# GQA decode attention with a small MLP on one core: all engines synchronized by hand in one section, TensorE's head groups in a loop, each loaded weight used by two matmuls

## The chip, the core and the metric

The kernel runs on one core of a Trainium2 chip. A core has TensorE (PE; its weight loads are counted apart, as PEld), VectorE (DVE), ScalarE (ACT), GpSimd (POOL), SyncE (SP, which here only issues DMAs), and 16 DMA engines that move data between HBM and the on-chip memory SBUF. The metric is the device time of one execution in microseconds (us). All runs quoted here are of the state called fast. A profile's span is about 1.8 us shorter than the time of the same execution, because it starts at the first instruction and ends with the last; times and spans are not mixed below.

## The reference, cut to what matters

```
B, Sq, D = 2, 1, 512
Hq, Hkv, Sk, Dh = 32, 8, 32768, 128            # 4 query heads share one K/V head
q = (x @ wq) ... ; scores = q . k * Dh**-0.5 ; p = softmax(scores) ; o = p . v
s = o.reshape(B, Sq, Hq * Dh) @ wo
g = silu(mlp(x))                                # small: 512 -> 1792 -> 512
return x + s * g
```

K and V hold 2 x 8 x 32768 x 128 bf16 elements each, 134 MB each. With wq, w3, w4 and wo the kernel must read 280.5 MB. There are 16 head groups (a batch and a K/V head), of 8.39 MB of K and 8.39 MB of V each. K arrives with its rows on the partitions; both kernels transpose it in SBUF on DVE before TensorE multiplies it with q (291.5 us of DVE in the kernel before).

## The kernel before

A framework places buffers in pools and derives the waits. K lies in a ring of three half-group slots, V in two. Per group there are two halves; each half takes eight transposes on DVE, 32 score matmuls, one exp, and 32 products with V. The finish of each group follows it at once.

```
kbuf = rings.tile([128, 3 * SLOT], BF16, name="kbuf")      # SLOT = 128 rows x 128, 32 KB a partition
vbuf = rings.tile([128, 2 * SLOT], BF16, name="vbuf")
...
for r in range(NR):                                        # emit_k: 8 chunks a half
    T = ktp.tile([128, W], I32, tag="T", name="T")         # 4 buffers of 1,024 words
    nc.vector.transpose(out=T..., in_=kt[:, r * W:(r + 1) * W]...)
    for nb in range(NB):
        for e in range(2):
            nc.tensor.matmul(sc[:, :], lhsT=z[:, nb, e, zc:zc + 128], rhs=Tb[:, nb, :, e], ...)
...                                                        # emit_v, last half of a group
nc.scalar.copy(out=ob[:, :], in_=o[:, :])
for t in range(VT):
    nc.tensor.matmul(oT[:, :], lhsT=ob[:, t * Dh:(t + 1) * Dh], rhs=sel_o[:, t, :], ...)
...                                                        # divide, select, put into oX
wo_parts = [(0, 4), (4, 7), (7, 8)]
for m in range(NG):
    eps = [emit_k(m, hs[0], True)]
    if not last: load_k(*groups[m + 1], ...)               # issued by SP
    eps.append(emit_k(m, hs[1], False))
    for i in range(NPART): emit_v(m, hs[i], i, eps[i])
    if not last: load_v(*groups[m + 1], ...)
    if m == NG - 2: ...                                    # wo, in wo_parts, behind the last K and V
```

The softmax here doesn't subtract the row's maximum and nothing guards it: scores larger than these inputs give would overflow.

## Time and profile before

| | before |
|---|---|
| time, median | 660.65 us (660.59 to 660.91, 3 runs) |
| span | 658.9 us |
| DMA | 280.91 MB, 426 GB/s over the span |
| PE busy, DVE busy | 59%, 53% |

These lines are from the page of the kernel before: busy time by engine, then the span in 40 slices (the digit is the busy share in tenths), then the busy share and the rate of the DMA engines in each slice, and the queues (queue, kind: packets, MB, share of 16 engines).

```profile
PE 386.7 (59%) x2652; PEld 172.1 (26%) x2684; DVE 346.0 (53%) x442; ACT 50.3 (8%) x152; POOL 6.9 (1%) x20
...
DMA  9999999999999999999999999999999999999995
GB/s 367 451 426 442 435 446 439 410 443 426 439 438 435 430 435 422 447 434 423 442 427 442 438 419 434 443 434 443 414 423 446 443 442 443 410 427 428 431 421 224
...
q1 hardware_dynamic: 6408, 280.50, 98.6%
q8 instruction: 21, 0.34, 0.2%
```

Read this as: no engine of the core is near full, the DMA engines are (9 tenths or more in every slice but the last). Queue 8 carries instructions, in 21 packets of 16 KB (below, "fetches").

The next lines are the chain of waits of the kernel before, in order of time (start, duration, what), cut to two groups and the end.

```profile
2.13 40.20 DMA kbuf<-in_A_k_cache_dram
...
51.51 29.45 DMA kbuf<-in_A_k_cache_dram
...
90.14 29.41 DMA kbuf<-in_A_k_cache_dram
...
613.66 39.09 DMA kbuf<-in_A_wo_dram
652.79 1.90 PE s_ps L400 x63
```

By these lines K tiles land at 42.33, 80.96 and 119.55 us, 38.6 us apart, which is 16.78 MB (K and V of a group) at about 434.6 GB/s. The end hangs on the load of wo, not on the last scores. The timeline of the finish (start, duration, instruction, in brackets the idle time before it and what ended that) shows why: the last V half is multiplied as soon as the last of its 16 completions is in (they come from 639.54 to 644.11 us, the products start at 644.15), the group's own finish is done at 650.2, and PE then waits for wo.

```profile
637.87 0.71 DVE L322 STREAM_TRANSPOSE pt<-ep 128x512 bf16<-128x512 bf16 x1 [1.87 <-ACT ep L320]
639.07 1.90 PE L343 MATMUL o<-vbuf,pt 128*16 128x512 bf16 x32
644.15 3.38 PE L343 MATMUL o<-vbuf,pt 128*16 128x512 bf16 x32 [3.18 <-DMA vbuf<-in_A_v_cache_dram]
650.01 0.17 DVE L372 TENSOR_REDUCE oX<-xm 128x4 bf16<-128x16 f32 x1
652.79 1.88 PE L400 MATMUL s_ps<-kbuf,oX 128*2 128x128 bf16 x64 [2.00 <-DMA kbuf<-in_A_wo_dram]
655.43 0.66 SPq L412 DMA_DIRECT2D out_dram<-out  x1
```

### The profile page before, as it was taken

The numbers are of one execution on the slowest core, as the hardware profiler recorded it, in microseconds if no ns is written. First come the engines' busy times: TensorE is split into PE (matmuls) and PEld (weight loads), VectorE is DVE, ScalarE is ACT, GpSimd is POOL, SyncE is SP. The second block draws the span as 40 slices with busy tenths as digits, with TensorE's granted clock in tenths as the row PEclk, the third lists the DMA queues.
The fourth block names the chain that finished last, engine by engine and source line by source line (L and its number), as shares of the span: only waits on it lengthen the run. The fifth ranks groups of instructions, "written<-read, shape, count | busy, mean of one in ns | idle before, by whom it ended". The sixth has DMA issues, their size and how long they took to land.

```text
span 658.9 us, 6323 instructions
## 1 busy us (share of the span) xinstructions
PE 386.7 (59%) x2652; PEld 172.1 (26%) x2684; DVE 346.0 (53%) x442; ACT 50.3 (8%) x152; POOL 6.9 (1%) x20
## 2 busy tenths in 40 slices
PE   2338194673828557283764729377482946738764
PEld 2313132231313223131331313123131322313322
DVE  5147192754809265381935629183572918447560
ACT  1301001010100101000010100101010010100000
POOL 4000000000000000000000000000000000000000
PEclk9999688786968968697886959878596877859896
DMA  9999999999999999999999999999999999999995
GB/s 367 451 426 442 435 446 439 410 443 426 439 438 435 430 435 422 447 434 423 442 427 442 438 419 434 443 434 443 414 423 446 443 442 443 410 427 428 431 421 224
DMA packets 6704, 280.91 MB, mean 426 GB/s; under 512 B 906, under 2 KB 916, under 8 KB 1940
## 3 DMA queue, kind: packets, MB, share of 16 engines
q1 hardware_dynamic: 6408, 280.50, 98.6%
q8 instruction: 21, 0.34, 0.2%
q0 software_dynamic: 256, 0.01, 0.0%
q14 instruction: 7, 0.06, 0.0%
q10 hardware_dynamic: 12, 0.00, 0.0%
HBM read 280.50 MB, written 0.00 MB: 426 GB/s over the span
## 4 chain that ended last, share of the span: by engine, by line
DMA 75%; DVE 14%; issue 7%; PE 3%; SPq 0%; ACT 0%; DVEq 0%
DMA kbuf<-in_A_k_cache_dram 69%; DVE T L303 14%; DMA kbuf<-in_A_wo_dram 6%; PE sc L311 2%; PE o L343 1%; PE s_ps L400 0%; ACT ep L320 0%; SPq L95 0%; DVE pt L322 0%; SPq L115 0%; SPq L392 0%; SPq L114 0%; SPq L101 0%; PE S L339 0%; DVE sg L408 0%
## 5 line engine op out<-in xcount | busy, mean ns | idle before, releaser
L311 PE MATMUL sc<-T,z 128*128 128x512 bf16 x992 | 276.4, 421 | 206.3 <-DVE T L303 197.8
L303 DVE STREAM_TRANSPOSE T<-kbuf 128x1024 int32<-128x1024 int32 x256 | 291.5, 1205 | 150.5 <-DMA kbuf<-in_A_k_cache_dram 150.5
L311 PEld LDWEIGHTS <-z 128*128 128x128 bf16 x1024 | 105.7, 103 | 371.2 <-issue 278.7
L343 PE MATMUL o<-vbuf,pt 128*16 128x512 bf16 x1024 | 69.9, 434 | 3.2 <-DMA vbuf<-in_A_v_cache_dram 3.2
L320 ACT ACTIVATE ep<-sc 128x512 bf16<-128x512 f32 x32 | 19.1, 597 | 493.2 <-PE sc L311 451.2
L334 DVE MEMSET o<- 128x512 f32 x16 | 7.8, 485 | 69.3 <-ACT ob L352 68.3
L322 DVE STREAM_TRANSPOSE pt<-ep 128x512 bf16<-128x512 bf16 x32 | 22.6, 707 | 34.7 <-ACT ep L320 34.4
L343 PEld LDWEIGHTS <-pt 128*16 128x16 bf16 x1024 | 27.2, 99 | 37.9 <-issue 18.2
L339 PE MATMUL S<-sm,ones_f 128*128 128x4 f32 x64 | 10.7, 238 | 26.1 <-DVE sm L338 26.1
L355 PE MATMUL oT<-sel_o,ob 128*128 128x4 f32 x128 | 16.9, 255 | 11.1 <-ACT ob L352 11.1
L355 PEld LDWEIGHTS oT<-sel_o,ob 128*128 128x128 f32 x128 | 15.5, 191 | 19.3 <-ACT ob L352 19.3
L339 PEld LDWEIGHTS S<-sm,ones_f 128*128 128x128 f32 x64 | 10.7, 188 | 30.9 <-DVE sm L338 28.4
L352 ACT COPY ob<-o 128x512 f32<-128x512 f32 x16 | 9.4, 586 | 83.4 <-PE o L343 83.4
L362 DVE TENSOR_TENSOR on<-oT,rec 128x4 bf16<-128x4 f32 x16 | 2.6, 162 | 21.8 <-PE oT L355 21.8
L286 ACT COPY z<-qr 32x16 bf16<-32x16 bf16 x64 | 12.6, 198 | 11.5 <-DVE qr L233 10.9
L360 DVE RECIPROCAL rec<-S 128x4 f32<-128x4 f32 x16 | 2.9, 182 | 7.6 <-PE S L339 7.6
L365 PEld LDWEIGHTS <-sel_r 128*128 128x128 bf16 x64 | 5.2, 117 | 5.2 <-issue 5.2
L320 ACT ACTIVATION_READ_ACCUMULATOR ep<-sc 128x1 f32 x32 | 6.3, 198 | 0.2
L215 PE MATMUL qT_ps<-xT,kbuf 128*128 128x2 bf16 x128 | 3.6, 165 | 4.5 <-DMA kbuf<-in_A_wq_dram 4.5
L365 PE MATMUL xp<-on,sel_r 128*128 128x4 bf16 x64 | 3.8, 164 | 4.1 <-DVE on L362 4.1
L338 DVE TENSOR_SCALAR sm<-sel_h,rs 128x4 f32<-128x4 f32 x32 | 6.0, 188 | 0.0
L370 DVE TENSOR_TENSOR xm<-xp,mask 128x16 f32<-128x16 f32 x16 | 2.8, 174 | 5.3 <-PE xp L365 5.3
(64 smaller groups left out, 48.5 us busy)
## 6 DMA issues: line engine op xcount, KB each, us to landing
kbuf<-in_A_k_cache_dram SPq DMA_DIRECT2D x2, 4096.0 KB, 29.1
vbuf<-in_A_v_cache_dram SPq DMA_DIRECT2D x2, 4096.0 KB, 26.7
kbuf<-in_A_wq_dram SPq DMA_DIRECT2D x1, 4096.0 KB
vbuf<-in_B_w_dram SPq DMA_DIRECT2D x2, 1792.0 KB, 21.6
kbuf<-in_A_wo_dram SPq DMA_DIRECT2D x1, 2048.0 KB, 35.9
kbuf<-in_A_wo_dram SPq DMA_DIRECT2D x1, 1536.0 KB, 39.1
kbuf<-in_A_wo_dram SPq DMA_DIRECT2D x1, 512.0 KB
kbuf<-in_A_k_cache_dram SPq DMA_DIRECT2D x15, 29.4
```

Of the source, the lines that this page charges most:

```text
L286: nc.scalar.copy(out=z[32 * j:32 * j + 32, :, :, c:c + rep], in_=qr[32 * j:32 * j + 32, :, :, b, g * rep:(g + 1) * rep],)
L303: nc.vector.transpose(out=T[:, :].rearrange("p (b t k) -> p t b k", b=NB, t=RT), in_=kt[:, r * W:(r + 1) * W].rearrange("p (t b k) -> p t ...
L311: nc.tensor.matmul(sc[:, :], lhsT=z[:, nb, e, zc:zc + 128], rhs=Tb[:, nb, :, e], start=(r == 0 and nb == 0 and e == 0), stop=(r == NR - 1 ...
L320: nc.scalar.activation(out=ep[:, :], in_=sc[:, :], func=ACT.Exp, scale=inv_sqrt_dh, accum_out=rs[:, :])
L322: nc.vector.transpose(out=pt[:, :, :].rearrange("p r (t h) -> p t r h", h=rep), in_=ep[:, :].rearrange("p (t r h) -> p t r h", r=NR, h=rep),)
L334: nc.vector.memset(state["o"][:, :], 0.0)
L338: nc.vector.tensor_scalar_mul(out=sm[:, :], in0=sel_h[:, :], scalar1=rs[:, 0:1])
L339: nc.tensor.matmul(S[:, :], lhsT=ones_f[:, :], rhs=sm[:, :], start=(i == 0), stop=(i == NPART - 1))
L343: nc.tensor.matmul(o[32 * j:32 * j + VT * rep, :], lhsT=pt[:, r, a * VT * rep:(a + 1) * VT * rep], rhs=vt[:, u * VT:(u + 1) * VT, :].rearr ...
L352: nc.scalar.copy(out=ob[:, :], in_=o[:, :])
L355: nc.tensor.matmul(oT[:, :], lhsT=ob[:, t * Dh:(t + 1) * Dh], rhs=sel_o[:, t, :], start=(t == 0), stop=(t == VT - 1),)
L365: nc.tensor.matmul(xp[:, r, :], lhsT=sel_r[:, r, :, :].rearrange("p j w -> p (j w)"), rhs=on[:, :], start=True, stop=True,)
```

## The change

The intent is fewer instructions and fewer weight loads. The kernel is rewritten as one section in which every wait is written by hand. PE's work for the first 15 groups becomes a loop of 197 instructions. One transpose covers 2,048 words, one exp covers a whole group, and a loaded weight serves two matmuls. The group's output is masked and reduced on DVE (collect), and the selection sums over all groups are done once, behind the last group's scores. wo comes in four parts. The diff rewrites nearly the whole file; its core:

```
-    kbuf = rings.tile([128, 3 * SLOT], BF16, name="kbuf")
+    kbuf = stile([128, 3 * UNIT], BF16, "kbuf")           # now the first buffer of the program
+    T = [stile([128, W], I32, f"T{i}") for i in range(2)] # 2 buffers of 2,048 words
...
+    with nc.Fori(1, NG, engines=bass.OrderedEngineSet([PE]), head_slot={PE: 0}) as i:
+        nc.tensor.wait_ge(s_z, i)
+        for n in range(NR):
+            nc.tensor.wait_ge(s_T[n], i)
+            emit_chunk(n)            # 4 x (ldweights, then 2 matmuls that use it)
+        nc.tensor.wait_ge(s_pt, i)
+        nc.tensor.wait_ge(s_v[0], i * 16)
+        pe.done(emit_v(0, NU))
...
+    for m in range(NL):              # NL = 15
+        k_read = scores(m)           # transposes, exp, transpose of p; issues K(m + 1)
+        t_ob.append(collect(m, t_v(m)))   # DVE: mask multiply and reduce, 128x1024
+        sp.wait(t_v(m))
+        V.append(load_v(m + 1))
...
+    for n in range(NR):              # the last group
+        pe.wait((s_T[n], NG))
+        emit_chunk(n)
+    scores(m)
+    t_sm = weigh(0, NL)
+    t = sums(0, NL, t_sm, t_ob[-1], ...)   # PE: 1 + 15 f32 matmuls
+    t_on = divide(0, NL, t, ...)
+    t_sm = weigh(NL, NG)
+    pe.wait(t_pt[-1], V[m][0])
+    emit_v(0, NU // 2)
...
-    wo_parts = [(0, 4), (4, 7), (7, 8)]
+    wo_parts = [(0, 2), (2, 5), (5, 7), (7, 8)]
```

## The prediction

> **What bounds it now.** The DMA stream. The page shows DMA at 9 tenths or more in every slice but the last; its chain of waits is 75% DMA; PE is busy 59%, DVE 53%. In the chain of waits K tiles land every 38.6 us (42.35, 80.98, 119.57, ...): 16.78 MB (K and V of one head group) per 38.6 us = 434.6 GB/s. The packet records agree: 64 KB takes 2,418 ns on one of 16 engines. [...] 280.5 MB at that rate is an estimated 646 us of 658.9. The queue never runs dry: the next K is issued 9 us after K lands, with about 10 us of V still in flight. So only the head, the tail and time lost inside the stream can move.
>
> **Lost time.** The packet records show 21 instruction fetches of 16 KB on queue 8, and some of 8 KB on queue 14. Each 16 KB fetch (about 0.9 us) also lengthens that DMA engine's next data packet by about 0.5 us: 1.4 us on one engine. Engines are hit two or three times, and a load is complete only when its slowest engine is. The spread between first and last engine grows from 0.63 us (first load) to 4.5 us (last V). [...]
>
> **What the change does.**
> - PE's program falls from 5,090 to 700 instructions as built[...]. DVE falls from 662 to 252. Nearly all fetches vanish: the last V lands near 640 to 641 us instead of 643.7, wo near 650 instead of 652.8: -2.8 us, all on the critical path.
> - Halved weight loads (105.7 us in L311, 27.2 us in L343), wider transposes and exps: less PE, DVE and ACT work, none on the path: 0.
> - T has two buffers of 2,048 columns, not four of 1,024: K's first half is read in 10 to 12 us, inside V's 19.3 us. No new wait.
> - Tail: after wo's landing 16 matmuls (about 0.5 us) are left in place of 64 (1.9 us): -1.3 us. The last group's finish gains DVE work (mask multiply and reduction over 128x1024, about 1.1 us each, estimated from the trace's 128x512 and 128x1024 instructions): 9 us after V lands against 6.5, but wo comes 9 us after V: a near tie.
> - [...]
>
> Sum: 660.65 - 2.8 - 1.3 + 0.6 = about 657.1 us, 0.5% faster.
>
> **Predicted: 657.1 us, 80% range 654.5 to 660.5; faster by over 2%: 0.01; within 2%: 0.96; slower by over 2%: 0.03.**
>
> **What would show it.** Right: K landings 38.6 us apart without the present outliers (39.0 to 39.8); queue 8 nearly empty; DMA 9 everywhere; last V at 640 to 641 us; about 0.5 us of PE between wo and the last products; PEld clearly lower, to no effect. Wrong: idle DMA slices in mid-span, or waits of the DMA queue on DVE or PE over 19 us.
>
> **What would make it wrong.** [...] If each of 15 back-edges refetched on one DMA engine, 15 x 1.4 = 21 us would be lost (slower by 3%). Or the loop's waits stall PE by over 10 us per group. Or the last group's finish overtakes wo: 1 to 2 us.

The sum came to 657.1 us. The term of +0.6 us in it, for the section's entry and exit, is cut from the list above it, because it named no trace that it came from; the terms that remain, -2.8 and -1.3 us, make 656.55 us. That the loop would be fetched only once was the assumption, and no trace had shown it; the fetches that the runs below show are 4 with the loop and 14 with it written out. "Hit two or three times" fits the 16 completions of the last V half in the kernel before: seven come from 639.54 to 640.05 us, five about 2.7 us later and four about 4.3 us later, where two and three fetches of 1.4 us make 2.8 and 4.2. The 21 us for refetching back-edges are an estimate from the 1.4 us that a fetch held one DMA engine in the kernel before.

## The result, and the profile after

The time after is 663.63 us median (662.26 to 664.40, 4 runs), against 660.78 us (660.59 to 660.94, 4 runs) of the kernel before in the same rounds. The ratio is 1.0041, 95% interval 1.0024 to 1.0058: within 2%, but clearly slower. A ratio here is the mean time of one kernel's fast runs over the mean of the other's of the same rounds, so it is not quite the ratio of the medians. The predicted 657.1 us, and the range up to 660.5 us, missed.

The same lines of the page, for the changed kernel:

```profile
PE 371.3 (56%) x2328; PEld 81.4 (12%) x1336; DVE 372.9 (56%) x234; ACT 37.2 (6%) x104; POOL 1.4 (0%) x8
...
DMA  8999999999999999999999999999999999999993
GB/s 363 457 418 432 448 440 440 436 404 436 436 448 440 436 404 436 444 414 462 436 408 436 444 440 412 460 408 440 436 444 440 410 430 436 440 444 410 438 407 154
...
q1 hardware_dynamic: 7144, 280.50, 98.3%
q8 instruction: 4, 0.07, 0.0%
```

Weight loading halved (172.1 to 81.4 us) and the instruction packets fell from 21 to 4, as intended. The DMA engines are still full up to the last slice. The issuing queue did wait longer: these lines (what SP waited for: us in total, times, longest us) are from the kernel before and then from the changed kernel.

```profile
SPq L86 <- DVE T L303: 136.9, 15, 9.1
SPq L95 <- PE o L343: 106.0, 15, 8.4
...
SPq L178 <- PE o L182: 286.3, 15, 23.1
SPq L178 <- DVE T L512: 284.0, 15, 24.8
```

The prediction had named waits on DVE or PE over 19 us as a sign that it was wrong. They occurred (24.8 and 23.1 us) and left no idle slice in the DMA row, so they did not stop the stream. So where did the time go? The finish answers half of it. These are lines of the timeline of the changed kernel (start, duration, instruction, and in brackets the idle time before it and what ended that):

```profile
606.44 1.02 ACT L521 ACTIVATE ep<-sc 128x1024 bf16<-128x1024 f32 x1 [44.90 <-PE sc L182]
609.10 5.12 PE L182 MATMUL o<-vbuf,pt 128*32 128x512 bf16 x64 [2.69 <-DVE pt L528]
614.26 1.23 DVE L536 TENSOR_TENSOR om<-o,mask 128x1024 f32<-128x1024 f32 x1 [5.31 <-PE o L182]
615.52 1.87 DVE L541 TENSOR_REDUCE ob<-om 128x128 f32<-128x1024 f32 x1
617.32 4.49 DVE L512 STREAM_TRANSPOSE T<-kbuf 128x2048 int32<-128x2048 int32 x2
...
639.67 1.25 DVE L528 STREAM_TRANSPOSE pt<-ep 128x1024 bf16<-128x1024 bf16 x1 [3.34 <-ACT ep L521]
641.34 5.10 PE L560 MATMUL pB<-sel_h,ob 128*128 128x4 f32 x30
646.38 3.53 PE L182 MATMUL o<-vbuf,pt 128*32 128x512 bf16 x32
650.06 1.90 PE L182 MATMUL o<-vbuf,pt 128*32 128x512 bf16 x32
653.26 1.87 DVE L541 TENSOR_REDUCE ob<-om 128x128 f32<-128x1024 f32 x1
656.46 1.43 PE L601 MATMUL pD<-kbuf,oX 128*2 128x128 bf16 x48
658.58 0.65 SPq L178 DMA_DIRECT2D out_dram<-out  x1
```

In this profile's chain of waits no DMA stands after 604 us; from there it runs through PE, DVE and ACT alone, by the instructions shown. The last V half landed near 642.8 us, but its products could only start at 650.06, because PE was busy with the 30 passes of the selection sums (5.10 us) and then with the first V half (3.53 us). Both ran while the clock granted to TensorE (1.00 is full speed) was low: 0.65 over the sums and 0.53 over the first V half, against 1.00 over the second, equal, half, which took 1.90 us. The output is issued at 658.58 us, against 655.43 before.

The packet records of the two traces give the other half. I tabulated them: the instruction packets, the share of all 64 KB packets that took exactly 2,418 ns, the mean of what a 64 KB packet took above that (over all that started from 45 to 600 us, those at 2,418 ns included, those delayed by 100 ns or more left out), and when the last packet of V and of wo ended.

```
                 16 KB fetches  64 KB packets at 2,418 ns  mean extra  last V ends  last wo ends  from there to the end of the span
before                      21                        98%      0.15 ns    643.72 us     653.68 us                           5.25 us
after                        4                        23%      3.60 ns    642.75 us     652.93 us                           8.83 us
```

So the stream ended 0.75 us earlier, not the 2.8 us predicted, although the fetches went. About four in five of the 64 KB packets became a few ns longer. And what comes after the stream took 3.6 us more. These are two separate questions.

### The profile page after: what moved, and what is told of

Same layout as the page of the kernel before. It is cut to its first block, busy times and chain, and to the rows that moved or that the text cites. A ratio compares the mean times of both kernels' runs of the same rounds, so it can differ in the third digit from the quotient of the medians.

```text
span 661.8 us, 4221 instructions
## 1 busy us (share of the span) xinstructions
PE 371.3 (56%) x2328; PEld 81.4 (12%) x1336; DVE 372.9 (56%) x234; ACT 37.2 (6%) x104; POOL 1.4 (0%) x8
## 4 chain that ended last, share of the span: by engine, by line
DMA 50%; DVE 30%; PE 16%; issue 2%; ACT 1%; SPq 0%
DMA kbuf<-in_A_k_cache_dram 50%; DVE T L512 25%; PE sc L182 10%; PE o L182 4%; DVE ob L541 2%; DVE pt L528 1%; DVE om L536 1%; ACT ep L521 1%; PE pB L560 1%; PE pD L601 0%; SPq L178 0%; PE pA L557 0%; DVE sg L650 0%; DVE out L652 0%; PE pC L575 0%
## 5 line engine op out<-in xcount | busy, mean ns | idle before, releaser
L182 PE MATMUL sc<-T,z 128*128 128x512 bf16 x992 | 270.7, 418 | 205.6 <-DVE T L512 204.4
L512 DVE STREAM_TRANSPOSE T<-kbuf 128x2048 int32<-128x2048 int32 x128 | 285.3, 2282 | 110.0 <-DMA kbuf<-in_A_k_cache_dram 85.4
L182 PE MATMUL o<-vbuf,pt 128*32 128x512 bf16 x1024 | 80.5, 484 | 56.7 <-DMA vbuf<-in_A_v_cache_dram 29.8
L445 PEld LDWEIGHTS <-z 128*128 128x128 bf16 x512 | 52.6, 103 | 423.2 <-issue 313.3
L536 DVE TENSOR_TENSOR om<-o,mask 128x1024 f32<-128x1024 f32 x16 | 19.6, 1224 | 95.2 <-PE o L182 95.2
L528 DVE STREAM_TRANSPOSE pt<-ep 128x1024 bf16<-128x1024 bf16 x16 | 19.9, 1245 | 53.4 <-ACT ep L521 53.4
L521 ACT ACTIVATE ep<-sc 128x1024 bf16<-128x1024 f32 x16 | 16.4, 1023 | 575.5 <-PE sc L182 575.5
L462 PEld LDWEIGHTS <-pt 128*32 128x32 bf16 x512 | 16.2, 119 | 119.2 <-issue 84.9
L541 DVE TENSOR_REDUCE ob<-om 128x128 f32<-128x1024 f32 x16 | 29.9, 1871 | 0.5
L560 PE MATMUL pB<-sel_h,ob 128*128 128x4 f32 x32 | 5.5, 303 | 2.5 <-DVE ob L541 2.5
## 6 DMA issues: line engine op xcount, KB each, us to landing
kbuf<-in_A_k_cache_dram SPq DMA_DIRECT2D x12, 4096.0 KB, 23.1
```

Of the source, the lines that this page charges most:

```text
L182: return nc.tensor.add_instruction(mybir.InstMatmult(name=nc.get_next_instruction_name(), engine=PE, ins=[nc.tensor.lower_ap(rhs), nc.tens ...
L445: nc.tensor.ldweights(w, tile_position=(0, 0))
L462: nc.tensor.ldweights(weights(u0 + j), tile_position=(0, 32 * j))
L512: t = dve.done(nc.vector.transpose(out=T[n % 2][:, :].rearrange("p (b t k) -> p t b k", b=NB, t=NF * RT), in_=kbuf[:, a:a + 2 * W].bitcast ...
L521: t = act.done(nc.scalar.activation(out=ep[:, :], in_=sc[:, :, :].rearrange("p f c -> p (f c)"), func=ACT.Exp, scale=inv_sqrt_dh, accum_ou ...
L528: t_pt.append(dve.done(nc.vector.transpose(out=pt[:, :, :].rearrange("p r (q h) -> p q r h", h=rep), in_=ep[:, :].rearrange("p (q r h) -> ...
```

## The experiments

Theory A: the loss is in the finish, which PE and DVE now set (the late sums above all). Theory B: the loss is the stretched packets. For the stretch itself there are four suspects: the loop with its waits against a register, the phases in which the DMA engines run, the K loads that are split in halves more often, and the place of the buffers. A fifth, contention with the engines for SBUF, is unlikely by the first trace of the changed kernel: the mean extra is 3.50 ns for packets that overlap a DVE transpose of K and 3.73 ns for those that do not.

The runs came in three sets, each with its own runs of the kernel before.

### Control: the changed kernel again

No edit.

> Control: the changed kernel again. About 663.6 us, 0.4% over before. Its packets are a few ns longer than in before (mean of the 64 KB packets from 45 to 600 us 3.6 ns over 2,418). If that stretch is a fixed property of this program it shows here again with about the same mean; if it depends on the phases in which the DMA engines happen to run, it differs.

Measured: 662.12 us (661.96 to 664.68), ratio 1.0031. The packets: 23% at 2,418 ns, mean extra 3.60 ns, the same as in the first trace to two digits. So the stretch comes back with the program. The times scatter over nearly 3 us, where the kernel before keeps within 0.4 us. The two traces of the changed kernel show one source: the 64 products of the last-but-one V took 5.12 us in the first and 3.63 us in the second, and all behind them moved by about as much (the output is issued at 657.15 instead of 658.58 us). This is the second trace's line:

```profile
609.15 3.63 PE L182 MATMUL o<-vbuf,pt 128*32 128x512 bf16 x64 [2.69 <-DVE pt L528]
```

The work is the same; the granted clock over it was 0.70 in the first trace and 1.00 in the second. This is what a finish set by PE looks like: it varies with the granted clock. In the kernel before, whose finish the DMA sets, the last V half took 3.38 us at a granted clock of 0.55, and PE still waited for wo behind it (2.00 us, up to 652.79), so that low clock did not move the end.

### The sums ahead of the last group's scores

```
-    scores(m)
-    t_sm = weigh(0, NL)
-    t = sums(0, NL, t_sm, t_ob[-1], ...)
+    t_sums = sums(0, NL, t_sm, t_ob, ...)    # now waits for each group's ob in turn
     pe.wait((s_z, NG))
     for n in range(NR): ...
+    scores(m)                                # weigh(0, NL) now follows scores(NL - 1)
```

> The selection sums of the first 15 head groups (1 + 15 f32 matmuls, 5.1 us on PE) go ahead of the last group's scores instead of behind them; no other change. Theory A (the loss is the serial finish: these sums stand between the last scores and the last V products): the finish is again bound by wo's landing, about 659 us (658 to 660), faster than before. Theory B (the loss is that every DMA packet is stretched and the stream is later): no gain, 663 us.

Measured: 659.58 us (659.37 to 659.85), ratio to before 0.9982. The changed kernel had 662.12 us in the same rounds. Theory A holds: moving 5 us of PE work into PE's idle time took 2.5 us off. PE is again waiting for wo at the end, as in the kernel before, and the scatter is gone. The timeline of this run:

```profile
614.79 3.47 PE L560 MATMUL pB<-sel_h,ob 128*128 128x4 f32 x30
640.26 1.25 DVE L528 STREAM_TRANSPOSE pt<-ep 128x1024 bf16<-128x1024 bf16 x1 [3.34 <-ACT ep L521]
641.56 1.90 PE L182 MATMUL o<-vbuf,pt 128*32 128x512 bf16 x32 [2.61 <-DVE pt L528]
643.62 1.90 PE L182 MATMUL o<-vbuf,pt 128*32 128x512 bf16 x32
653.11 0.60 PE L601 MATMUL pD<-kbuf,oX 128*2 128x128 bf16 x16 [0.18 <-DMA kbuf<-in_A_wo_dram]
654.41 0.65 SPq L178 DMA_DIRECT2D out_dram<-out  x1
```

The sums now run while DVE collects the last-but-one group and begins on the last K, the V halves follow each other at once, and the last 16 products wait for wo. The granted clock over the sums and over both V halves was 1.00 here, and they took 3.47 us and 1.90 us each. The mean extra of the packets is still 3.57 ns.

### The early sums, with PE's loop written out

```
-    with nc.Fori(1, NG, engines=bass.OrderedEngineSet([PE]), head_slot={PE: 0}) as i:
+    for i in range(1, NG):                   # plain unrolling: waits against constants
```

> As the early-sums kernel, with PE's loop written out 15 times, so that the instruction fetches come back (about 3,500 instructions) and the waits are against constants. Fetch theory: 8 or more fetches on queue 8, the spread of the DMA engines at the last V over 3 us again, wo later by 1 to 2 us, time 1 to 2 us above the early-sums kernel. If fetches do not matter: the same time. If the waits against a register stretch the packets: packets back at 2,418 ns and the stream earlier by about 1 us before the fetches are counted.

Measured: 660.87 us (660.77 to 660.97), 1.3 us above the early-sums kernel of the same rounds. There are 14 fetches instead of 4; the DMA engines' completions of the last K are up to 3.5 us apart instead of 1.9, and the last wo packet ends at 654.12 us instead of 652.66. So fetches do cost time in a stream that is never idle: 1.3 us for ten of them. The stretch stays (3.51 ns), so neither the loop nor the waits against a register make it.

### The kernel before with wo in four parts

```
-    wo_parts = [(0, 4), (4, 7), (7, 8)]
+    wo_parts = [(0, 2), (2, 5), (5, 7), (7, 8)]
```

> The kernel before with wo loaded in the four parts of the changed kernel instead of three, nothing else. Prediction's tail step: after the last part only 16 matmuls are left instead of 64, so -1.3 us: about 659.4 us. If the part before the last lands just as late as the last: 660.5 us or more.

Measured: 660.54 us (660.34 to 660.56) against 660.91 us; ratio 0.9994, interval 0.9977 to 1.0011. The medians differ by 0.4 us and no run is below 660.34; the interval, which reaches to 1.5 us faster, would alone not rule out 1.3. The packet records say why little was to be gained: the last wo packet of the kernel before ends at 653.68 us, 0.9 us after the wait that the timeline shows at 652.79. That wait was for the second part; the wait for the third is hidden inside the 64 products that follow it as one row.

### The early sums, with K and V at multiples of 512 bytes

```
+    stile([128, 192], BF16, "pad")           # 384 bytes a partition
     kbuf = stile([128, 3 * UNIT], BF16, "kbuf")
```

In the built programs the K and V buffers start 128 bytes past a multiple of 512 in the changed kernel, and at a multiple of 512 in the kernel before. No trace shows these addresses; the runs with pads agree with them.

> The early-sums kernel with a pad of 384 bytes ahead of the K buffer, so that the K and V buffers start at multiples of 512 bytes in each partition (in the changed kernel at 128 past one; in the kernel before at a multiple of 512). Nothing else. Alignment theory (a destination off a 256-byte boundary costs each packet a few ns): 64 KB packets back at 2,418 ns, mean extra under 0.5 ns instead of 3.6, last wo landing and time about 1 us earlier than the early-sums kernel (658.6 us). If the stretch comes from the loop, the waits, the split K loads or the phases of the DMA engines: mean extra 3.5 ns as before, same time.

Measured: 658.03 us (657.87 to 658.31), against 659.71 us of the unaligned kernel (next) and 660.82 us of the kernel before in the same rounds. 92% of the packets are at 2,418 ns, and the last wo packet ends at 651.72 us instead of 652.94. The mean extra is 2.19 ns, more than the 0.5 I expected: few packets, but longer ones (236, started between 103 and 266 us, 28 ns longer on average), in an execution that was the slowest of the five (658.31 us). The time fell by 1.7 us, more than the 1 us expected. This version beats both kernels: its ratio to the kernel before is 0.9957, interval 0.9943 to 0.9971. Lines of its timeline: the last V half is multiplied when it lands, the last group's output is ready, and PE waits for the last part of wo.

```profile
642.12 1.90 PE L183 MATMUL o<-vbuf,pt 128*32 128x512 bf16 x32 [1.57 <-DMA vbuf<-in_A_v_cache_dram]
650.29 0.18 DVE L592 TENSOR_REDUCE oX<-xm 128x4 bf16<-128x16 f32 x1
652.05 0.60 PE L602 MATMUL pD<-kbuf,oX 128*2 128x128 bf16 x16 [0.22 <-DMA kbuf<-in_A_wo_dram]
```

### The early-sums kernel again

No edit; for the comparison on the same chip.

> The early-sums kernel again, for a comparison with the aligned one on the same chip: 659.6 us, mean extra of 64 KB packets 3.6 ns.

Measured: 659.71 us (659.67 to 659.82), ratio 0.9983, mean extra 3.58 ns.

### The kernel before, its K and V moved by 128 bytes

```
+    rings.tile([128, 64], BF16, name="pad")  # 128 bytes a partition
     kbuf = rings.tile([128, 3 * SLOT], BF16, name="kbuf")
```

> The kernel before with a pad of 128 bytes ahead of the K buffer, so that its K and V buffers stand 128 bytes past a multiple of 512. Nothing else. Alignment theory: mean extra of the 64 KB packets about 3.5 ns, time +0.9 to +1.2 us (about 661.9 us). Rivals: packets at 2,418 ns, time as before.

Measured: 662.59 us (662.42 to 662.71), +1.8 us, ratio 1.0025 (1.0011 to 1.0039). 31% of the packets at 2,418 ns, mean extra 3.44 ns; the last wo packet ends at 655.42 us, 1.7 us later. The stretch appears in the old kernel with nothing changed but the place of the two buffers and of what is allocated behind them. The alignment theory is shown in both directions.

### The kernel before, moved by 256 bytes and by 64 bytes

The same edit with a pad of 128 and of 32 elements.

> The kernel before with its K and V buffers 256 bytes past a multiple of 512. If the boundary that counts is 256 bytes: packets at 2,418 ns and the time of before, 660.8 us. If it is 512: as with 128 bytes, 662.6 us.

Measured: 660.80 us (660.47 to 660.89) against 660.77 us, ratio 0.9999; 99% of the packets at 2,418 ns. So the boundary that counts is 256 bytes, not 512.

> The kernel before with its K and V buffers 64 bytes past a multiple of 512. [...] the same stretch as with 128 bytes (mean extra about 3.5 ns, 662.6 us). If the cost grows with the offset: about half.

Measured: 662.75 us (662.48 to 662.76), ratio 1.0028; 11% at 2,418 ns, mean extra 3.65 ns. 64 bytes off costs as much as 128, so of these two offsets it is the missed boundary that costs, not the distance. These runs show the boundary. They show neither a cost that grows with the offset nor why the boundary costs, so the mechanism stays open.

### The changed kernel with the aligned buffers alone

The same pad of 384 bytes, the late sums left in place.

> The changed kernel with the 384 byte pad alone (K and V buffers at multiples of 512), its late sums left as they are. Both causes are separate: packets at 2,418 ns, last V about 1 us earlier, but the end is set by the serial finish, which starts from K and V tiles that land 0.8 to 1 us earlier: 662 to 663 us, so a gain of 0.5 to 1.5 us and still above before. If alignment were the whole loss: below 660.8 us.

Measured: 662.78 us (660.60 to 663.23), ratio 1.0022 (1.0003 to 1.0042). 98% of the packets at 2,418 ns, mean extra 0.09 ns, with the K loads split as before, so the split is no cause of the stretch either. The last V ends at 641.32 us and the last wo at 651.28 us: 1.4 and 1.7 us earlier than in the first trace of the changed kernel, 1.6 and 1.9 us earlier than in the control. Over packets of all sizes, a DMA engine's data packets took 648.69 us here and 650.18 us in the first trace, on average over the 16 engines: 1.5 us, of which the 64 KB packets make 0.7, those of 32 KB 0.5, and the 4 KB packets of wo 0.3. So the 64 KB packets, whose mean extra is tabulated above, are only about half of the cost. The time did not follow: it is between the two medians of the changed kernel (662.12 and 663.63), so a gain cannot be told from its scatter. From the last wo packet to the end are 9.51 us. An earlier stream brought no gain that can be seen while PE and DVE set the finish; that answers theory B.

### The early sums without shared weights

```
-                nc.tensor.ldweights(w, tile_position=(0, 0))
                 for f in range(NF):
-                    inst = matmul_loaded(sc[:, f, :], w, Tb[:, nb, f, :, e], ...)
+                    inst = nc.tensor.matmul(sc[:, f, :], lhsT=w, rhs=Tb[:, nb, f, :, e], ...)
```

and the same in the products with V.

> The early-sums kernel with every matmul of the loop and of the last group loading its own weights (so 1,984 weight loads in those two stages instead of about 1,000), that is without the sharing of a loaded weight. Prediction: weight loads are off the critical path, so PE's weight-load time about doubles (81 to about 170 us) and the time stays at that of the early-sums kernel within 0.5 us. [...] if back-edges then refetch, queue 8 shows over 15 fetches and the time rises by over 1 us; [...] 4 or 5 fetches as in the changed kernel.

Measured: 659.63 us (659.55 to 659.81), the same as the 659.71 us with sharing. Weight loading rose from 79.6 to 141.6 us (I expected about 170), the loads from 1,336 to 2,360, and the time did not move. So the sharing of loaded weights, the change's most visible part in the profile, is worth nothing here that these runs can see. The loop has about 261 instructions now instead of 197, and still there are only 5 fetches, so its back-edges did not refetch. A longer loop was not run.

Lines of this run's page:

```profile
PE 376.1 (57%) x2328; PEld 141.6 (22%) x2360; DVE 373.4 (57%) x234; ACT 37.2 (6%) x104; POOL 1.4 (0%) x8
q8 instruction: 5, 0.08, 0.1%
```

## Why the prediction was right or wrong, point by point

- **The bound: right.** In both kernels the DMA engines are full, and with aligned buffers 92 to 99% of the 64 KB packets take 2,418 ns in every kernel. What ends last in the changed kernel, though, is no longer the stream but PE and DVE (from 604 us on).
- **The fetches: the mechanism was right, the net size was not.** In the kernel before each 16 KB fetch holds one DMA engine for about 1.4 us (0.9 us of its own and 0.5 us on the next packet). The aligned changed kernel ends V at 641.32 us, 2.4 us before the kernel before (2.8 predicted), and writing the loop out costs 1.3 us for ten fetches. But in the changed kernel as it is, V ended at 642.75 us.
- **"Nearly all fetches vanish: the last V lands near 640 to 641 us": failed**, because the step took the packet time for granted. The rewrite moved the K and V buffers to 128 bytes off a 256-byte boundary. In place of 2,418 ns most 64 KB packets took a few ns more, and so did smaller ones: 1.7 to 1.8 us over the run, measured by taking it away (early sums, aligned) and by adding it to the kernel before (moved by 128 bytes).
- **Shared weights and wider operations worth 0: right for the weights**, shown by the run without sharing. The wider transposes and exps were not tested alone.
- **"No new wait": right in effect, but its sign failed.** SP's longest waits on DVE and PE grew from 9.1 and 8.4 to 24.8 and 23.1 us, beyond the 19 us that the prediction gave as a sign of being wrong. The DMA row keeps 9 all the same and K's first half was read in time, so these waits cost nothing and 19 us was the wrong bound.
- **"After wo's landing 16 matmuls are left in place of 64: -1.3 us": failed.** I took a wait for the second part of wo for the wait for the last. The last part lands 0.9 us later, behind products that are already running. The kernel before with four parts gained 0.4 us, which its interval does not separate from zero.
- **"The last group's finish ... 9 us after V lands ... a near tie": failed, and this is the main loss.** I listed the added DVE work but not the 30 f32 passes of the sums that stand on PE between the last scores and the V products. They took 5.10 us, at a granted clock of 0.65, and delayed both V halves, the first of which took 3.53 us at 0.53. The last group's output was ready at 656.99 us, 14.2 us after the last V, not 9. The reduction was also under-sized (1.87 us, not 1.1). With the sums moved, the chain is what I had costed: in the aligned early-sums kernel the last group's output is ready at 650.5 us, 8.7 us after the last V, and wo is waited for. That 8.7 comes so near to the costed 9 is partly luck, since one term was under-sized and one wait for a part of wo lies inside it.
- **Entry and exit +0.6 us: mis-sized.** The first packet comes 0.2 us later (1.97 against 1.76 us), and the stretch from the issue of the output to the end is 0.3 us shorter (3.18 against 3.51 us).
- **The fear of refetching back-edges: unfounded here.** 4 fetches with the loop of 197 instructions, and 5 with one of about 261.

The sum: the stream's end moved by -0.75 us (about -2.4 from fetches and the rest, +1.7 from alignment), what follows it by +3.6 us; together +2.8 us of span, as measured (658.94 to 661.76 us). With both faults mended the kernel takes 658.03 us, inside the predicted range.

Left open: the stretch does not set in from the first load. In the changed kernel the loads of wq, w3 and w4 go to buffers that are just as unaligned, and most of their packets take what they take with aligned buffers (1,213 ns for 32 KB, 535 ns for 14 KB); so do K's first 64 KB packets (2,418 ns). The first that are a few ns longer start at 38.9 us, after the first instruction fetch (33.3 us); in the kernel before moved by 128 bytes they start at 22.1 us, again after the first fetch (19.0 us). From 65 us on four in five of the changed kernel are longer. Whether the fetches set it off, no run tells. Also open is why the aligned early-sums kernel has its 236 longer packets where the aligned changed kernel has next to none; only one execution of each was profiled.

## What to carry to other kernels

When a kernel is bound by one unbroken DMA stream, count what disturbs the stream (instruction fetches, here 1.3 us for ten; the start address of the big buffers, here 1.8 to 2.0 us of 660.8 in the kernel before with them 64 or 128 bytes off, nothing to be seen with 256) before counting what the engines save; put the big buffers at multiples of 256 bytes and check this in the built program after every rewrite of the allocation. Then draw the finish as a list in each engine's program order, with every instruction that stands between the last data and the output: work that is gathered "once at the end" leaves the idle time in the middle, where it was free, and lands on the one stretch that is not, where PE's time also varies with the granted clock (5.10 us for the sums at 0.65, 3.47 at 1.00). In a timeline, a row of many instructions can hide a second wait, so look at when the last packet really ended.
